# A decode step with sliding-window attention and an MLP gate: the order of the last output rows, one wide row, and 80 VectorE rows in the last key stage

## The chip, the cores and the metric

The kernel runs on one core of a Trainium2 chip. The metric is the device time of one execution in microseconds. The engines are named as the profile names them: PE is TensorE, DVE is VectorE, ACT is ScalarE, POOL is GpSimd, SP is SyncE, which issues nearly all the transfers.

## The reference, cut to what matters

One token is decoded (B = S = 1, D = 512). It is normalised, goes through attention over the last 4096 positions of 32 heads of 128, and the result is gated by a small MLP branch.

```
xn = layernorm(x)                                   # 1 x 512
q  = (xn @ wq) as 32 heads of 128
k, v = k_cache[:, :, -4096:], v_cache[:, :, -4096:]  # 32 x 4096 x 128, bf16
p  = softmax(q . k / sqrt(128))                      # per head
o  = p @ v                                           # 32 x 128
s  = o as 1 x 4096, @ wo                             # wo is 4096 x 512
h  = gelu(layernorm(xn) @ w1), its four quarters shifted along the sequence, @ w2
x1 = xn + h
g  = silu(x1 + gelu(layernorm(x1) @ w3) @ w4)        # w3 512 x 1376, w4 1376 x 512
out = x + s * g
```

With a sequence of one token the shifted quarters are all zero, so w1 is not read. Keys and values are 32 MiB each and are read once.

## The kernel before, in words

The 32 heads are worked in 8 groups of 4 (`G`). A group's keys are one tile of 128 partitions: partition b*4+a holds 128 consecutive positions of head a, 32 KB. The values lie the same way. Keys have three buffers, values two. The loop runs over stages s = 0 to 9: stage s loads and scores the keys of group s and works the values of group h = s - 2 (`LAG`). All loads go over SP's one queue in program order (`load`, line 79); a load of keys or values waits until the group that last used its buffer has been read. PE, DVE and ACT work strictly in the order in which the program lists their instructions (a manual schedule).

**Scores.** Of the 128 positions in each partition, DVE scores the first `nd(g)` and PE the rest. DVE does it in four parts (`k_vector`): a product with the broadcast query (L301) and a sum over 128 (L303). PE turns the other columns in batches of up to 8 (`k_turn`, L317), ACT copies each batch out of PSUM (L319), and PE multiplies with the query (`k_scores`, L325). `sm_own` picks each head's own score on ACT (L334); `sm_max` sums these on DVE (L339) and takes the maximum per partition (L341). `sm_turn` turns the maxima (L347 on PE; L349, L351 on DVE make `md`), and `sm_exp` broadcasts the result (L356, L359) and takes the exponentials on ACT (L363). `nd` is

```
return 64 if g < EARLY or g >= LATE else 80
```

with EARLY = 2 and LATE = 7, so group 7, whose stage is the last with keys, has 64 columns on DVE.

**Values.** `v_part` multiplies 128 columns of values with the probabilities (L423, 128 small matmuls for a group; groups 0 and 2 in another form, L415). `v_out` divides by the sum (L442 for the last two groups, L446 for others).

**Output rows.** Multiplication with wo is done in three blocks: heads 0 to 15, 16 to 23 and 24 to 31. For blocks 0 and 1 wo is loaded with eight or sixteen consecutive rows in each partition, and `ox_spread` (L453), `ox_pick` (L461, L463, L467) rearrange the attention output to match. Block 0 is a wide row (`y_wide`): 16 matmuls of 512 columns into one partition (L489), in stage 6, copied by ACT to `y_row` (L492). Block 1 is 32 narrow matmuls (`y_block` calls `rows_add`, L150), each of 128 columns[...], added up in `y_ps`. `y_row` is added to `y_ps` by `rows_add` with a one as the weight. Of the last block, 320 rows are loaded in the rearranged way into a tile of 40 used partitions (`wo_few`; `ox_few`, L473 and L476, makes its weights `of`) and the rest head by head (`wo_rows`, `y_head`).

Stage 8 closes group 7's softmax, does block 1 and `y_row`, then group 6's values, and prepares `of`. Stage 9 takes group 7's values, loaded in three pieces by `cuts = (0, 64, 112, CP)`: the first piece, then the few rows and heads 26 and 27, then the other two pieces, then heads 28 to 31. The last two DVE instructions are the gate (L602) and the residual (L604).

**MLP weights.** `w4_sb` is loaded in three transfers: 8 rows in each partition, then 2, then 96 single rows; `chunks` selects the columns of `w3_sb` to match, with steps of 8, 2 and 1.

Of the kernel before, what the change touches and what calls it, by code (L numbers as in the profile page):

```python
# [8 lines left out]
P = 128  # L9
# [3 lines left out]
ALU = mybir.AluOpType  # L13
# [8 lines left out]
NE = 5  # L22
V_BUFS = 2
EARLY = 2
LATE = 7
MOVED = (0, 2)


# [1 line left out]
def kernel(  # L30
# [14 lines left out]
    nc = tc.nc  # L45
# [9 lines left out]
    CP = G * W // P  # L55
    PB = P // G
    KC = D // P
    F = B_w3.shape[1]
    assert F == 8 * P + 2 * P + 96
    scale = float(Dh) ** -0.5  # L60


# [15 lines left out]
    def load(dst, src):  # L78
        return tc.keep_in_program_order(nc.sync.dma_start(out=dst, in_=src))
# [8 lines left out]
    w3_sb = wts.tile([P, KC, F], BF16, name="w3_sb")  # L88
    load(w3_sb[:], B_w3.rearrange("(p c) n -> p c n", p=P))
    w4_sb = wts.tile([P, 11, D], BF16, name="w4_sb")  # L90
    load(w4_sb[:, 0:8, :], B_w4[0:8 * P, :].rearrange("(p c) n -> p c n", p=P))
    load(w4_sb[:, 8:10, :], B_w4[8 * P:10 * P, :].rearrange("(p c) n -> p c n", p=P))
    load(w4_sb[0:96, 10, :], B_w4[10 * P:F, :])
    wq_sb = wts.tile([P, KC, HD], BF16, name="wq_sb")
    load(wq_sb[:], A_wq.rearrange("(p c) n -> p c n", p=P))
# [1 line left out]
    def load_kv(pool, cache, g, cuts=(0, CP)):  # L97
        t = pool.tile([P, CP, Dh], BF16, tag="kv", name="kv")
        src = cache[0, G * g:G * g + G, W0:, :].rearrange("a (b c) d -> b a (c d)", b=PB)
        dst = t[:].rearrange("p c d -> p (c d)")  # L100
        for c0, c1 in zip(cuts, cuts[1:]):
            load(dst[:, c0 * Dh:c1 * Dh], src[:, :, c0 * Dh:c1 * Dh])
        return t
# [9 lines left out]
    one_f = ones_f[0:1, 0:1]  # L113
# [33 lines left out]
    def rows_add(ps, col, w, last):  # L147
        k = col.shape[0]
        for j in range(KC):
            nc.tensor.matmul(ps[32 * j:32 * j + 1, :], lhsT=col, rhs=w[0:k, j * P:(j + 1) * P],  # L150
                             start=False, stop=last, skip_group_check=True)
# [49 lines left out]
    nc.vector.tensor_scalar(out=xn_row[:], in0=x_row[:], scalar1=negmean[:], scalar2=rstd[:],  # L201
                            op0=ALU.add, op1=ALU.mult)

    chunks = [(P, slice(r, 8 * P, 8)) for r in range(8)]
    chunks += [(P, slice(8 * P + r, 10 * P, 2)) for r in range(2)]
    chunks += [(96, slice(10 * P, F, 1))]
    a_ps = ps_misc.tile([P, 11], FP32, tag="misc", name="a_ps")
    for j, (m, cols) in enumerate(chunks):
# [50 lines left out]
    for c in range(2):  # L259
        nc.vector.tensor_copy(  # L260
            out=few[:, c, 0:4 * NE].rearrange("p (a b) -> p a b", b=4),
# [6 lines left out]
    y_ps = ps_y.tile([P, P], FP32, name="y_ps")  # L268
# [7 lines left out]
                            op=ALU.max)  # L276
    par_t = const.tile([1 + G, PB, G], FP32, name="par_t")
    nc.vector.tensor_scalar(out=par_t[:],
                            in0=ident_f[0:1 + G, 1:1 + G].unsqueeze(1).to_broadcast([1 + G, PB, G]),
# [7 lines left out]
    def nd(g):  # L287

        return 64 if g < EARLY or g >= LATE else 80

# [110 lines left out]
    def load_rows(h, n):  # L401
        if h == h_part:
            load(wo_rows[r_part:P, 0, :], A_wo[h * P + r_part:(h + 1) * P, :])
            h, n = h + 1, n - 1
        load(wo_rows[:, h - h_part:h - h_part + n, :],
             A_wo[h * P:(h + n) * P, :].rearrange("(h p) n -> p h n", p=P))
# [3 lines left out]
    def v_part(g, v, c0=0, c1=CP):  # L410
        s = st[g]
        if g in MOVED:
            s["ov"] = ps_o.tile([4 * G, 4, Dh], FP32, tag="oT", name="ov")
            for c in range(0, CP, 4):
                nc.tensor.matmul(s["ov"][:], lhsT=s["pT"][:, c:c + 4, :].rearrange("p i a -> p (i a)"),  # L415
                                 rhs=v[:, c:c + 4, :], start=(c == 0), stop=(c == CP - 4))
            s["ov_sb"] = sm_pool.tile([4 * G, 4, Dh], FP32, tag="ov_sb", bufs=1, name="ov_sb")
            nc.scalar.copy(out=s["ov_sb"][:], in_=s["ov"][:])  # L418
            return
        if c0 == 0:  # L420
            s["oT"] = ps_o.tile([P, G], FP32, tag="oT", name="oT")
        for c in range(c0, c1):
            nc.tensor.matmul(s["oT"][:], lhsT=v[:, c, :], rhs=s["pT"][:, c, :], start=(c == 0),  # L423
                             stop=(c == CP - 1))
# [46 lines left out]
    def ox_few(i):  # L471
        of_ps = ps_misc.tile([64, 8], FP32, tag="misc", name="of_ps")
        nc.tensor.matmul(of_ps[:], lhsT=few[:].rearrange("p a b -> p (a b)"), rhs=ox_blk[i][:],  # L473
                         start=True, stop=True)
        of = sm_pool.tile([64, 8], BF16, tag="of", bufs=1, name="of")
        nc.vector.tensor_copy(out=of[:], in_=of_ps[:])  # L476
        ox_blk[i] = of


    y_row = small.tile([1, D], FP32, name="y_row")  # L480

    yr = {}

    def y_wide(i, t0, t1):
        n = blocks[i][1]
        if t0 == 0:
            yr[i] = ps_tr.tile([1, D], FP32, tag="pt", name="yr_ps")
        for t in range(t0, t1):
            nc.tensor.matmul(yr[i][:], lhsT=ox_blk[i][:, t:t + 1], rhs=wo_blk[i][:, t, :], start=(t == 0),  # L489
                             stop=(t == n - 1))  # L490
        if t1 == n:
            nc.scalar.copy(out=y_row[:], in_=yr[i][:])  # L492

    def y_block(i):
        for t in range(8):
            rows_add(y_ps, ox_blk[i][:, t:t + 1], wo_blk[i][:, t, :], False)
# [2 lines left out]
        rows_add(y_ps, o_blk[few_block][:, h - few_h:h - few_h + 1], wo_row(h), h == H - 1)  # L499

    NG = H // G
    cuts = (0, 64, 112, CP)
    region = tc.manual_schedule(engines={mybir.EngineType.PE, mybir.EngineType.DVE,
                                         mybir.EngineType.Activation})
    region.__enter__()
    v_pool = None
    for s in range(NG + LAG):
        h = s - LAG
        last = h == NG - 1
        kn = load_kv(k_pool, A_k_cache, s, (0, 64, CP) if s == 0 else (0, CP)) if s < NG else None  # L510
        if s == LAG:
            wts_guard.__exit__(None, None, None)
            v_pool = ctx.enter_context(tc.tile_pool(name="v", bufs=V_BUFS))
            wo_blk[few_block] = v_pool.tile([64, 8, D], BF16, tag="wo_few", bufs=1, name="wo_few")
            nc.gpsimd.memset(wo_blk[few_block][:], 0.0)
            wo_rows = v_pool.tile([P, H - h_part, D], BF16, tag="wo_rows", bufs=1, name="wo_rows")
            nc.gpsimd.memset(wo_rows[0:r_part, 0, :], 0.0)
        if last:
            load_rows(h_part, 2)
            v = load_kv(v_pool, A_v_cache, h, cuts)  # L520
            for r, n in ((H - G, 2), (H - 2, 1), (H - 1, 1)):
                load_rows(r, n)
        elif h >= 0:
            v = load_kv(v_pool, A_v_cache, h)
        if h == 3:
            wo_24 = k_pool.tile([P, 32, D], BF16, tag="kv", name="wo_24")
            wo_blk[0], wo_blk[1] = wo_24[:, 0:16, :], wo_24[:, 16:24, :]
            load_wo(0)
        if h == 5:
            load_wo(1)  # L530
            load_few()

        if s < NG:
            nb = len(batches(s))

            def keys(b0, b1):
                for b in range(b0, b1):
                    k_turn(s, kn, b)
                    if b > 0:
                        k_scores(s, b - 1)  # L540

            k_open(s)
            k_vector(s, kn, 0)
            keys(0, 2)
            if s > 1:
                sm_den(s - 2)
                sm_rden(s - 2)
            if h - 1 in MOVED:
                v_add(h - 1)
                v_out(h - 1)  # L550
            keys(2, 4)
            k_vector(s, kn, 1)
            if s > 0:
                sm_turn(s - 1)
            if s == 6:
                ox_spread(0)
            keys(4, nb)
            k_scores(s, nb - 1)
            sm_own(s)
            if s > 0:  # L560
                sm_exp(s - 1)
            k_vector(s, kn, 2)
            if s == 6:
                ox_pick(0)
            k_vector(s, kn, 3)
            if h >= 0:
                v_part(h, v)
            sm_max(s)
            if s == 6:
                y_wide(0, 0, 16)  # L570
            if h >= 0 and h not in MOVED:
                v_out(h)
        elif s == NG:

            sm_den(NG - 2)
            sm_rden(NG - 2)
            sm_turn(NG - 1)
            ox_spread(1)
            sm_exp(NG - 1)
            ox_pick(1)  # L580
            y_block(1)
            rows_add(y_ps, one_f, y_row, False)
            v_part(h, v)
            v_out(h)
            ox_spread(few_block)
            sm_den(NG - 1)
            sm_rden(NG - 1)
            ox_pick(few_block)
            ox_few(few_block)
        else:  # L590
            v_part(h, v, 0, cuts[1])
            y_block(few_block)
            for r in range(h_part, H - G):
                y_head(r)
            for c0, c1 in zip(cuts[1:], cuts[2:]):
                v_part(h, v, c0, c1)
            v_out(h)
            for r in range(H - G, H):
                y_head(r)
# [36 lines left out]
```

## Time and profile before

| | |
|---|---|
| median of 9 runs | 194.66 us (194.46 to 195.64) |
| the profiled execution, its own time | 194.64 us |
| its span in the profile | 192.8 us |
| busy: PE, PE weight loads, DVE, ACT | 133.0, 101.6, 145.9, 85.8 us |
| read from HBM | 78.84 MB |
| mean granted PE clock | 0.685 |

The span is the time from the first to the last instruction in the profile; the 1.84 us by which the time is longer lie around it. A stage's work can be found in the timeline by the line numbers above: the last stage with keys (7) runs on DVE from 155.35 to about 170.5 us, stage 8 follows to 183.2, and stage 9 ends with L604 at 190.2 and the transfer of the output.

### The profile page before, as it was taken

Reading aid. Unit: us, or ns where it says so; the run is one execution under the profiler, and the core shown is the slowest. Engines: PE = TensorE matmul, PEld = TensorE weight load, DVE = VectorE, ACT = ScalarE, POOL = GpSimd, SP = SyncE. Lnnn points to the kernel's source line nnn. Section 1 sums busy time; section 2 is a strip of 40 time slices with the busy share of each in tenths; the row PEclk is TensorE's granted clock in tenths of the full one; section 3 lists DMA queues with packets and bytes.
Section 4 is the critical chain, followed back from the end, with each engine's and each line's share of the span. In section 5 each row is a group of like instructions: output and inputs, shape, how many; then the busy total and the mean of one; then the engine's idle time right before and its main releaser. Section 6 shows DMA issues by size and latency. Waiting matters only on the chain.

```text
span 192.8 us, 4716 instructions
## 1 busy us (share of the span) xinstructions
PE 133.0 (69%) x2098; PEld 101.6 (53%) x2098; DVE 145.9 (76%) x160; ACT 85.8 (45%) x193; POOL 6.5 (3%) x14
## 2 busy tenths in 40 slices
PE   0549763977726579778595994981788878754792
PEld 0444363866625433477584344881768257742781
DVE  1550208999999999999999999995899999950201
ACT  2003002888896360558276322771475077841000
POOL 2110008000000000000000000000000000000000
PEclk9999955589765557985558798555566696755555
DMA  5999999999999999999999999999999999999980
GB/s 187 419 476 435 398 428 432 423 428 432 435 432 435 435 430 432 435 435 435 432 432 435 428 432 404 466 435 425 421 425 437 425 435 398 449 416 396 411 336 18
DMA packets 4869, 79.13 MB, mean 410 GB/s; under 512 B 682, under 2 KB 1482, under 8 KB 1866
## 3 DMA queue, kind: packets, MB, share of 16 engines
q1 hardware_dynamic: 4698, 78.84, 96.0%
q8 instruction: 16, 0.26, 0.5%
q10 hardware_dynamic: 152, 0.00, 0.0%
q14 instruction: 3, 0.02, 0.0%
HBM read 78.84 MB, written 0.00 MB: 409 GB/s over the span
## 4 chain that ended last, share of the span: by engine, by line
DVE 42%; DMA 36%; PE 13%; ACT 5%; issue 1%; SPq 0%; ACTq 0%
DMA kv<-in_A_k_cache_dram 27%; DVE S L303 25%; DVE prod L301 14%; DMA kv<-in_A_v_cache_dram 7%; ACT kt L319 4%; PE oT L423 4%; PE pt L317 4%; PE yr_ps L489 3%; DMA x_bf<-in_A_x_dram 2%; PE sT L325 2%; PE y_ps L150 1%; DVE S L339 1%; DVE m L341 1%; DVE mx L349 1%; ACT own L334 0%
## 5 line engine op out<-in xcount | busy, mean ns | idle before, releaser
L303 DVE TENSOR_REDUCE S<-prod 128x20 f32<-128x2560 bf16 (+1 forms) x32 | 83.8, 2620 | 1.1
L319 ACT COPY kt<-pt 128x1024 bf16<-128x1024 bf16 x54 | 53.1, 1015 | 24.0 <-PE pt L317 23.4
L317 PE MATMUL pt<-ident_bf,kv 128*128 128x128 bf16 x432 | 45.8, 276 | 10.0 <-DMA kv<-in_A_k_cache_dram 7.9
L301 DVE TENSOR_TENSOR prod<-kv,q_bc 128x2560 bf16<-128x2560 bf16 (+1 forms) x32 | 44.3, 1385 | 5.5 <-DMA kv<-in_A_k_cache_dram 2.8
L317 PEld LDWEIGHTS <-kv 128*128 128x128 bf16 x432 | 36.8, 126 | 12.3 <-DMA kv<-in_A_k_cache_dram 8.8
L325 PE MATMUL sT<-qT_bf,kt 128*128 128x4 bf16 x432 | 20.1, 168 | 17.1 <-ACT kt L319 16.4
L325 PEld LDWEIGHTS <-kt 128*128 128x128 bf16 x432 | 16.8, 104 | 24.3 <-ACT kt L319 23.9
L423 PEld LDWEIGHTS <-kv 128*128 128x128 bf16 x768 | 21.0, 104 | 4.8 <-DMA kv<-in_A_v_cache_dram 4.8
L423 PE MATMUL oT<-pT,kv 128*128 128x4 bf16 x768 | 21.5, 166 | 2.9 <-DMA kv<-in_A_v_cache_dram 2.8
L415 PE MATMUL ov<-kv,pT 128*16 128x512 bf16 x64 | 18.1, 453 | 0.0
L363 ACT ACTIVATE pT<-S,mb 128x128 bf16<-128x128 f32 x32 | 13.9, 571 | 0.3
L415 PEld LDWEIGHTS <-pT 128*16 128x16 bf16 x64 | 6.4, 103 | 10.7 <-issue 5.5
L442 DVE TENSOR_TENSOR o<-oT,rden 128x4 bf16<-128x4 f32 x2 | 0.3, 162 | 13.5 <-PE oT L423 13.5
L334 ACT ACTIVATE own<-sT,par 128x48 f32<-128x48 f32 (+1 forms) x32 | 7.6, 358 | 3.6 <-PE sT L325 3.6
L446 ACT ACTIVATE o<-oT,rden 128x1 bf16<-128x1 f32 x24 | 4.3, 260 | 9.4 <-PE oT L430 5.8
L363 ACT ACTIVATION_READ_ACCUMULATOR pT<-S,mb 128x1 f32 x32 | 8.2, 257 | 0.0
L418 ACT COPY ov_sb<-ov 16x512 f32<-16x512 f32 x2 | 1.2, 576 | 14.1 <-PE ov L415 14.1
L224 DVE COPY hr<-hr_ps 1x512 f32<-1x512 f32 x1 | 0.7, 679 | 8.5 <-PE hr_ps L221 8.5
L356 PE MATMUL mb_ps<-md,par_t 5*128 5x4 f32 x16 | 3.9, 314 | 2.9 <-DVE md L351 2.2
L489 PE MATMUL yr_ps<-wo,ox 128*1 128x512 bf16 x16 | 5.0, 479 | 1.1 <-DVE ox L467 1.1
L213 ACT ACTIVATE a_bf<-a_ps 128x10 bf16<-128x10 f32 x1 | 0.2, 180 | 12.0 <-PE a_ps L210 12.0
L347 PE MATMUL mt_ps<-ident_f,m 128*1 128x128 f32 x8 | 2.8, 351 | 3.7 <-DVE rden L374 3.7
(113 smaller groups left out, 91.5 us busy)
## 6 DMA issues: line engine op xcount, KB each, us to landing
kv<-in_A_k_cache_dram SPq DMA_DIRECT2D x7, 4096.0 KB, 31.8
kv<-in_A_v_cache_dram SPq DMA_DIRECT2D x7, 4096.0 KB, 31.2
wq_sb<-in_A_wq_dram SPq DMA_DIRECT2D x1, 4096.0 KB, 18.0
kv<-in_A_k_cache_dram SPq DMA_DIRECT2D x2, 2048.0 KB, 21.5
wo<-in_A_wo_dram SPq DMA_DIRECT2D x1, 2048.0 KB, 30.7
kv<-in_A_v_cache_dram SPq DMA_DIRECT2D x1, 2048.0 KB, 13.3
kv<-in_A_v_cache_dram SPq DMA_DIRECT2D x1, 1536.0 KB, 16.4
w_sb<-in_B_w_dram SPq DMA_DIRECT2D x1, 1376.0 KB, 7.0
```

Source lines behind the costliest of these rows:

```text
L301: nc.vector.tensor_tensor(out=prod[:, 0:m, :], in0=kn[:, rows, :], in1=q_bc[:, g:g + 1, :].to_broadcast([P, m, Dh]), op=ALU.mult)
L303: nc.vector.tensor_reduce(out=st[g]["S"][:, rows], in_=prod[:, 0:m, :], axis=AX.X, op=ALU.add)
L317: nc.tensor.transpose(pt[:, c - c0, :], kn[:, c, :], ident_bf[:])
L319: nc.scalar.copy(out=kts[b][:, 0:c1 - c0, :], in_=pt[:, 0:c1 - c0, :])
L325: nc.tensor.matmul(st[g]["sT"][:, c - nd(g), :], lhsT=kt[:, c - c0, :], rhs=qT_bf[:, G * g:G * g + G], start=True, stop=True)
L334: nc.scalar.mul(s["own"][:, 0:m, a], s["sT"][:, 0:m, a], par[:, a:a + 1])
L356: nc.tensor.matmul(mb_ps[:], lhsT=par_t[:].rearrange("k b a -> k (b a)"), rhs=md[:], start=True, stop=True)
L363: nc.scalar.activation(out=s["pT"][:, :, a], in_=s["S"][:], func=ACT.Exp, scale=scale, bias=mb[:, a:a + 1], accum_out=s["sum"][:, a:a + 1])
L415: nc.tensor.matmul(s["ov"][:], lhsT=s["pT"][:, c:c + 4, :].rearrange("p i a -> p (i a)"), rhs=v[:, c:c + 4, :], start=(c == 0), stop=(c == ...
L423: nc.tensor.matmul(s["oT"][:], lhsT=v[:, c, :], rhs=s["pT"][:, c, :], start=(c == 0), stop=(c == CP - 1))
L446: nc.scalar.mul(o_blk[b][:, c + k:c + k + 1], st[g]["oT"][:, k:k + 1], st[g]["rden"][:, k:k + 1])
L489: nc.tensor.matmul(yr[i][:], lhsT=ox_blk[i][:, t:t + 1], rhs=wo_blk[i][:, t, :], start=(t == 0), stop=(t == n - 1))
```

## The change

Three things are done, beside a change of form in two places.

- LATE becomes 8: group 7 has 80 columns on DVE and 48 on PE, as groups 2 to 6 have.
- Block 1 (heads 16 to 23) is done by `y_wide` in place of `y_block`: 8 matmuls of 512 columns. DVE adds its result to `y_row`. The rows of `y_row` are added to `y_ps` after `ox_few`.
- In stage 9 the few rows and heads 26 and 27 stand ahead of all of group 7's values. `cuts` has one more entry, so that these are loaded and multiplied in four pieces (64, 32, 16, 16 columns).
- `w4` is loaded in two transfers, with 10 rows in each partition in place of 8 and 2.
- `load_kv(..., (0, CP))` spells out the default and changes nothing.

```diff
-LATE = 7
+LATE = 8
...
-    load(w4_sb[:, 0:8, :], B_w4[0:8 * P, :].rearrange("(p c) n -> p c n", p=P))
-    load(w4_sb[:, 8:10, :], B_w4[8 * P:10 * P, :].rearrange("(p c) n -> p c n", p=P))
+    load(w4_sb[:, 0:10, :], B_w4[0:10 * P, :].rearrange("(p c) n -> p c n", p=P))
...
-    chunks = [(P, slice(r, 8 * P, 8)) for r in range(8)]
-    chunks += [(P, slice(8 * P + r, 10 * P, 2)) for r in range(2)]
+    chunks = [(P, slice(r, 10 * P, 10)) for r in range(10)]
...
-        if t1 == n:
+        if i == 0:
             nc.scalar.copy(out=y_row[:], in_=yr[i][:])
+        else:
+            nc.vector.tensor_tensor(out=y_row[:], in0=yr[i][:], in1=y_row[:], op=ALU.add)
...
-    cuts = (0, 64, 112, CP)
+    cuts = (0, 64, 96, 112, CP)
...
             ox_pick(1)
-            y_block(1)
-            rows_add(y_ps, one_f, y_row, False)
+            y_wide(1, 0, 8)
             v_part(h, v)
...
             ox_few(few_block)
+            rows_add(y_ps, one_f, y_row, False)
         else:
-            v_part(h, v, 0, cuts[1])
             y_block(few_block)
             for r in range(h_part, H - G):
                 y_head(r)
-            for c0, c1 in zip(cuts[1:], cuts[2:]):
+            for c0, c1 in zip(cuts, cuts[1:]):
                 v_part(h, v, c0, c1)
```

More of the change, by code (lines that the diff above doesn't have):

```diff
@@ L58 @@
     F = B_w3.shape[1]
-    assert F == 8 * P + 2 * P + 96
+    assert F == 10 * P + 96
     scale = float(Dh) ** -0.5
@@ L523 @@
         elif h >= 0:
-            v = load_kv(v_pool, A_v_cache, h)
+            v = load_kv(v_pool, A_v_cache, h, (0, CP))
         if h == 3:
```

## Prediction

> **What bounds the kernel now.** I read the page's slices first, then the chain of waits, then the timeline from 140 us on.
>
> ```profile
> DMA  5999999999999999999999999999999999999980
> ```
>
> The 16 DMA engines are full in every slice from the second to the last but one. 78.84 MB at the 430 GB/s or so of the middle slices is about 183 us, nearly the whole span: up to its last stages the kernel is its transfers, and work that only moves inside that stretch is free. What can be lost or won lies in the last 25 us. The chain of waits says of them:
>
> ```profile
> 169.64 13.35 DMA kv<-in_A_v_cache_dram
> ```
>
> This puts the last values (group 7) down to their issue at 169.64, when PE finished group 5's values and freed the buffer. The timeline shows why that is not the release:
>
> ```profile
> 149.31 0.58 SPq L79 DMA_DIRECT2D kv<-in_A_v_cache_dram  x1
> ...
> 169.80 0.41 DVE L339 TENSOR_REDUCE S<-own 128x64 f32<-128x256 f32 x1
> ...
> 173.32 1.02 PE L150 MATMUL y_ps<-wo,ox 128*1 128x128 bf16 x32 [0.62 <-DVE ox L467]
> ...
> 177.69 3.57 PE L423 MATMUL oT<-pT,kv 128*128 128x4 bf16 x128 [2.82 <-DMA kv<-in_A_v_cache_dram]
> ...
> 183.00 0.16 DVE L476 CAST of<-of_ps 64x8 bf16<-64x8 f32 x1 [0.26 <-PE of_ps L473]
> ...
> 183.04 1.87 PE L423 MATMUL oT<-pT,kv 128*128 128x4 bf16 x64
> 184.84 1.02 PE L150 MATMUL y_ps<-wo_few,of 64*1 64x128 bf16 x32
> ...
> 186.26 0.38 PE L150 MATMUL y_ps<-wo_rows,o 128*1 128x128 bf16 x7 [0.21 <-issue]
> ...
> 186.67 1.87 PE L423 MATMUL oT<-pT,kv 128*128 128x4 bf16 x64
> ...
> 188.79 0.69 PE L150 MATMUL y_ps<-wo_rows,o 128*1 128x128 bf16 x16 [0.26 <-DVE o L442]
> ```
>
> Group 6's values were issued at 149.31 and are used at 177.69, on landing: the queue runs some 28 us behind its issues, and group 7's pieces, issued 8 us before group 6 has landed, merely stand behind it. So PE is paced by landings: 177.69 (group 6), 183.04 (first piece of group 7) and 186.67 (second). The two margins that matter: PE has issued all of row block 1 (from 173.32, then y_row until 174.88) **2.8 us** before group 6 lands, and VectorE stands idle from 173.3 to 181.3.
>
> [...]
> 1. [...] at L489, the same wide form, the weight loads at 150.78, 151.20, 151.63 and 152.06 are 0.43 us apart, and the last nine matmuls take about 2.1 us.
> 2. [...] The windows of the trace agree, and show the half clock where the change puts its wide row:
>
> ```profile
> 149.70:153.20 3.50, 2.81 (x7) 0.85 (x8) 3.43 (x4) 0.00 (x0) 0.00 (x0) 0.51 1.05 445
> 153.20:155.40 2.20, 2.18 (x11) 0.70 (x10) 1.99 (x4) 0.02 (x1) 0.00 (x0) 1.00 0.93 402
> ...
> 169.60:173.30 3.70, 1.57 (x7) 1.03 (x6) 2.03 (x9) 1.70 (x10) 0.00 (x0) 0.50 0.98 414
> 173.30:177.70 4.40, 1.56 (x41) 0.84 (x41) 0.00 (x0) 0.93 (x6) 0.00 (x0) 0.50 0.98 378
> ```
>
> Columns: stretch, its length, busy time of PE, PE weight loads, DVE, ACT and POOL, granted clock, DMA share, GB/s.
> 3. [...] The 32 narrow ones of 173.32 take 1.02 us in all, and no matmul of the trace passes another: a late wide row holds up all behind it.
> [...]
>
> **The change, part by part.**
>
> *VectorE takes 80 rows in stage 7* (LATE 8). The four parts of 16 rows become four of 20, each a product and a sum:
>
> ```profile
> L303 DVE TENSOR_REDUCE S<-prod 128x20 f32<-128x2560 bf16 x20 | 56.4, 2820 | 0.7
> L301 DVE TENSOR_TENSOR prod<-kv,q_bc 128x2560 bf16<-128x2560 bf16 x20 | 29.7, 1484 | 2.8 <-DMA kv<-in_A_k_cache_dram 2.7
> L303 DVE TENSOR_REDUCE S<-prod 128x16 f32<-128x2048 bf16 x12 | 27.4, 2286 | 0.4
> L301 DVE TENSOR_TENSOR prod<-kv,q_bc 128x2048 bf16<-128x2048 bf16 x12 | 14.6, 1220 | 2.7 <-ACT q_bc L251 2.3 <-DMA kv<-in_A_k_cache_dram 0.2
> ```
>
> 4 x (2.820 - 2.286 + 1.484 - 1.220) = 3.19 us more. VectorE runs through this stage without a gap from 155.35 to 169.80, so all of it shows. The sum of own scores shrinks to the 48-row form (0.34 for 0.41 us): -0.07. Row maximum, turn, spread, pick and ox of block 1 hang on it in one line, so **row block 1 starts at 173.32 + 3.12 = 176.44**. PE and ACT lose 16 transposes, 16 score matmuls and two of eight kt copies (2 x 1.02 us of ACT). That releases group 5's values on PE (166.09 now): they next wait for md of group 6, which VectorE gives 1.6 us later, 164.5 for 162.86. They run some 1.3 us earlier, and so does the issue of group 7's values. I cost that at nothing: the cover is group 6 in the queue until 177.69. The exponentials of group 7 end near 177.4 instead of 174.2; first use at 183 or later.
>
> *Row block 1 as a wide row.* Gone: 32 narrow matmuls (1.02 us). New: 8 of 512 columns at the half clock, 8 x 0.427 = 3.42 us[...]. They end at 176.44 + 3.42 = **179.86**. Group 6's values, queued behind on PE and landed at 177.69, start 2.17 us late. On VectorE the add into y_row (1x512; nearest rows 0.57 us of ACT at L492, 0.68 at L224) stands at about 180.2 to 180.9, ahead of the output of group 6 (181.30 + 2.17 = 183.47): hidden. The y_row copy of stage 6 stays.
>
> *y_row's rows move* from 174.28 to behind ox_few. They are 8 small f32 matmuls, 0.60 us with their drain, and fall into the wait for the of cast. That cast ends at 183.16 + 2.17 = 185.33. What is left over pushes the few rows by 0 to 0.35 us (nothing if all fits in the wait, the rest of 0.60 if not); I take 0.10, so they start at 185.45.
>
> *The few rows and two heads go ahead of group 7's values.* These matmuls are the same. Now: 184.84 to 185.79 for the few rows, to 186.67 for the heads, of which about 0.24 is the wait for the second piece. Then all 128 matmuls of the values, which have mostly landed by then: 3.57 us as at 177.69. So 185.45 + 0.95 + 0.64 + 3.57 = **190.6, where it is 188.55 now: +2.06**. The gap of about 0.4 us inside the heads has no cause in the trace; it may go or stay, 0 to -0.4. Of the last four heads the last one starts only at 189.2 now, as its rows land last; with all rows landed some 0.1 us comes back. Sum: **+1.95 us**.
>
> *Queues.* The values come in four pieces for three, not five: one issue of about 0.6 us more at 169, hidden by the 8 us of queue. SP's last wo_rows issue starts at 177.7 now, as group 6 lands, eight transfers after it: an issue seems to wait for the landing eight back. With one more piece the last two do so. They would be out by 178.6 at the latest, 10 us before use: nothing. [...] The w4 load in one issue saves SP about 0.45 us at 2 us and 128 small packets, and strides L210's weights by 10 for 8: behind it wq and the keys are queued, so 0 to -0.1. POOL's instructions don't change.
>
> The profiled execution took 194.64 us (192.8 of span and 1.84 around it), the median of the runs shown is 194.66: no correction. **194.64 + 1.95 = 196.6 us.**
>
> **Rivals.**
> - *The wide row is quick* (PE at the full clock): 8 x 0.216 = 1.73 us, over at 178.17, +0.48 at group 6. By the same sum about +0.3: 194.95, no change that can be told. Against it: clock 0.50 from 169.6 to the end, and the L489 row started at the half clock though PE had just worked. Chance 0.04.
> - *VectorE's lateness is absorbed*, or the rows don't move: the wide row starts at 173.32, ends at 176.74, before 177.69. What is left is y_row's rows in the tail, against the wait for the second piece: 194.7. The decisive point is a delay under 0.95 us. Against it: VectorE has no gap in stage 7. Chance 0.03.
> - *Faster: the chain is right*, and group 7's landing is set by its issue. That comes 1.3 us earlier: 193.3. It decides only if the queue is empty at 169.6 and the wide row is over by 177.7. For it: the chain's 13.35 us step. Against it: the DMA share of 0.98 in both windows above. Chance 0.03.
> - *The lateness as summed*, 0.90: 195.9 to 197.2, [...] the push of 0 to 0.35, and the gap of 0 to -0.4.
>
> **How the numbers follow.** A measurement of this kernel can tell about 0.3%, 0.6 us, from no change. Slower takes the last case with a little off for its low end, 0.91; same takes the first two and that end, 0.06; faster 0.03. The range 195.7 to 197.2 leaves out the three rivals and the thin ends.
>
> **What would show it.** VectorE's last L339 at about 172.9; L489's second row from 176.4 to 179.9 at clock 0.50; PE's group 6 released by PE's own row, not by the DMA; the few rows from about 185.4; no DMA wait before group 7's last pieces; L442's last at about 190.6. Group 6's values at 177.7 would prove it wrong, and a wide row under 2 us would leave the first rival.

## The result, and the profile after

The changed kernel takes 196.36 us (median of 18 runs, 195.41 to 197.77), against 194.71 us for the kernel before (median of 55). The ratio is 1.0077, 95% interval 1.0060 to 1.0094: slower by about 1.5 us. The profiled execution took 196.65 us, 0.29 us over that median, with a span of 194.9. The changed kernel's line numbers are one or two lower: it runs L421 where the kernel before ran L423, L149 for L150, L487 for L489, L301 for L303.

The lines of the timeline that answer to those of before (start, duration, engine, line, operation; in brackets the idle time ahead of it and what ended that):

```profile
172.86 0.34 DVE L337 TENSOR_REDUCE S<-own 128x48 f32<-128x192 f32 x1
...
176.32 3.57 PE L487 MATMUL yr_ps<-wo,ox 128*1 128x512 bf16 x8 [0.62 <-DVE ox L465]
...
179.83 3.40 PE L421 MATMUL oT<-pT,kv 128*128 128x4 bf16 x128
179.93 0.68 DVE L492 TENSOR_TENSOR y_row<-yr_ps,y_row 1x512 f32<-1x512 f32 x1 [3.67 <-PE yr_ps L487]
...
184.87 0.16 DVE L474 CAST of<-of_ps 64x8 bf16<-64x8 f32 x1 [0.26 <-PE of_ps L471]
...
185.29 1.42 PE L149 MATMUL y_ps<-wo_few,of 64*1 64x128 bf16 x32
...
186.64 0.38 PE L149 MATMUL y_ps<-wo_rows,o 128*1 128x128 bf16 x8
...
186.95 3.67 PE L421 MATMUL oT<-pT,kv 128*128 128x4 bf16 x128
...
190.88 0.60 PE L149 MATMUL y_ps<-wo_rows,o 128*1 128x128 bf16 x16 [0.25 <-DVE o L440]
```

VectorE closes stage 7 at 172.86 instead of 169.80. The wide row starts at 176.32 and its eight matmuls take 3.57 us; group 6's values start at 179.83 with no wait for a transfer, where they waited 2.82 us for their landing before. From there the lateness goes through to the end: the gate starts at 191.53 us, where it started at 189.53. The windows of the trace, with the clock in the third column from the end, show the wide row at half clock (0.50) and the values after it at nearly full clock (0.96):

```profile
176.30:179.80 3.50, 3.48 (x8) 0.85 (x8) 0.00 (x0) 0.91 (x6) 0.00 (x0) 0.50 1.00 368
179.80:183.30 3.50, 3.50 (x131) 3.48 (x131) 0.71 (x2) 0.00 (x0) 0.00 (x0) 0.96 0.98 365
```

So far the trace reads as the prediction does. One line doesn't fit: the 32 matmuls of the few rows (L149, `wo_few`) take 1.42 us, where they took 1.02.

### The profile page after: what moved, and what is told of

The parts are those of the page before. It is cut to its first block, busy times and chain, and to the rows that moved or that the text cites. A ratio compares the mean times of both kernels' runs of the same rounds, so it can differ in the third digit from the quotient of the medians.

```text
span 194.9 us, 4601 instructions
## 1 busy us (share of the span) xinstructions
PE 136.7 (70%) x2042; PEld 100.8 (52%) x2042; DVE 149.6 (77%) x161; ACT 83.9 (43%) x191; POOL 6.4 (3%) x14
## 4 chain that ended last, share of the span: by engine, by line
DVE 50%; DMA 29%; PE 14%; ACT 4%; issue 1%; ACTq 0%; SPq 0%
DVE S L301 29%; DMA kv<-in_A_k_cache_dram 27%; DVE prod L299 16%; PE yr_ps L487 5%; PE oT L421 4%; ACT kt L317 3%; PE pt L315 2%; DMA x_bf<-in_A_x_dram 2%; PE y_ps L149 1%; PE sT L323 1%; DVE S L337 1%; DVE mx L347 1%; DVE m L339 1%; DVE ox L465 1%; DVE md L349 1%
## 5 line engine op out<-in xcount | busy, mean ns | idle before, releaser
L301 DVE TENSOR_REDUCE S<-prod 128x20 f32<-128x2560 bf16 (+1 forms) x32 | 86.0, 2686 | 1.1
L317 ACT COPY kt<-pt 128x1024 bf16<-128x1024 bf16 x52 | 51.2, 1014 | 23.7 <-PE pt L315 23.1
L299 DVE TENSOR_TENSOR prod<-kv,q_bc 128x2560 bf16<-128x2560 bf16 (+1 forms) x32 | 45.4, 1418 | 5.5 <-DMA kv<-in_A_k_cache_dram 2.8
L323 PE MATMUL sT<-qT_bf,kt 128*128 128x4 bf16 x416 | 19.3, 168 | 14.9 <-ACT kt L317 14.1
L323 PEld LDWEIGHTS <-kt 128*128 128x128 bf16 x416 | 16.1, 105 | 22.1 <-ACT kt L317 21.8
L421 PEld LDWEIGHTS <-kv 128*128 128x128 bf16 x768 | 20.8, 102 | 1.6 <-issue 1.1
L421 PE MATMUL oT<-pT,kv 128*128 128x4 bf16 x768 | 21.2, 166 | 0.1
L413 PE MATMUL ov<-kv,pT 128*16 128x512 bf16 x64 | 19.4, 478 | 0.0
L487 PE MATMUL yr_ps<-wo,ox 128*1 128x512 bf16 x24 | 10.1, 609 | 1.8 <-DVE ox L465 1.8
L487 PEld LDWEIGHTS <-ox 128*1 128x1 bf16 x24 | 2.7, 119 | 8.3 <-issue 6.0
L440 DVE TENSOR_TENSOR o<-oT,rden 128x4 bf16<-128x4 f32 x2 | 0.3, 162 | 8.3 <-PE oT L421 8.3
```

The source lines that it names most:

```text
L299: nc.vector.tensor_tensor(out=prod[:, 0:m, :], in0=kn[:, rows, :], in1=q_bc[:, g:g + 1, :].to_broadcast([P, m, Dh]), op=ALU.mult)
L301: nc.vector.tensor_reduce(out=st[g]["S"][:, rows], in_=prod[:, 0:m, :], axis=AX.X, op=ALU.add)
L317: nc.scalar.copy(out=kts[b][:, 0:c1 - c0, :], in_=pt[:, 0:c1 - c0, :])
L323: nc.tensor.matmul(st[g]["sT"][:, c - nd(g), :], lhsT=kt[:, c - c0, :], rhs=qT_bf[:, G * g:G * g + G], start=True, stop=True)
```

## The experiments

All ratios are to the kernel before, run on the same chip at the same time. The profiled executions of e4, f2, g1 and e7 took 1.1 to 1.7 us longer than the medians of their kernels, with all of the last stages later; their lines are read for waits, not for times.

### Undoing one part, doing one part

**All but the 80 rows** (e1), the changed kernel with

```diff
-LATE = 8
+LATE = 7
```

> The changed kernel with LATE = 7, so that VectorE takes 64 rows of the last keys as before; the wide row, the late y_row rows, the order of the last rows and the four pieces stay. Theory (the two delays share one margin of 2.8 us; either alone fits into it): the wide row runs from about 173.3 to 176.7 us, group 6's values start on their landing near 177.6, and the time is back at the kernel before, ratio 0.999 to 1.002. Rival 'tail' (the late end comes from the new order and the smaller packets of the last values, whose last rows land at 190.1 in the changed kernel against 189.2 before): the time stays at 1.005 to 1.009. Rival 'additive' (each part costs its own share): about half of the 1.6 us stays, 1.003 to 1.005.

Measured: 0.9992 (0.9972 to 1.0012), 194.63 us. The wide row was over before group 6 landed, and group 6 started on its landing:

```profile
172.99 3.57 PE L487 MATMUL yr_ps<-wo,ox 128*1 128x512 bf16 x8 [0.62 <-DVE ox L465]
177.52 3.58 PE L421 MATMUL oT<-pT,kv 128*128 128x4 bf16 x128 [0.95 <-DMA kv<-in_A_v_cache_dram]
```

The wide row, the order of the last rows, the four pieces and the w4 load together cost nothing, and gain nothing, while VectorE is on time. That ends the rival 'tail', which blames the new end by itself.

**The 80 rows alone** (e2), the kernel before with

```diff
-LATE = 7
+LATE = 8
```

> The kernel before with LATE = 8 alone. Theory: VectorE is 3.1 us late, block 1 as narrow rows starts at 176.4 and with y_row is issued by 178.0, so group 6's values start about 0.3 us late; ratio 1.000 to 1.003. Rival 'additive': VectorE's 3.1 us cost about half of the loss, 1.004 or more. Rival 'tail': 1.000, VectorE does not matter.

Measured: 1.0053 (1.0033 to 1.0074), 196.01 us. That is more than my theory allowed, and within the range of the rival 'additive'; but e1, where that rival expected 1.003 to 1.005, speaks against it.

**The change with narrow rows** (e3), the changed kernel with

```diff
-            y_wide(1, 0, 8)
+            y_block(1)
```

> The changed kernel with block 1 as 32 narrow matmuls again in place of the wide row (y_row then holds block 0 alone, its rows are still added after ox_few); 80 rows on VectorE and the new tail stay. Theory: block 1 starts at 176.3 and is issued by 177.4, before group 6 lands near 177.6; ratio 0.999 to 1.002. Rival 'additive': 1.003 to 1.005. Rival 'tail': 1.005 to 1.009.

Measured: 1.0078 (1.0055 to 1.0101), 196.51 us: no better for taking away the very thing that the prediction blames.

**The wide row alone** (e4), the kernel before with `y_wide(1, 0, 8)` in place of `y_block(1)`, VectorE's add, and y_row's rows after `ox_few`.

> The kernel before with the wide row alone (added to y_row by VectorE; y_row's rows moved behind ox_few, as in the change), 64 rows on VectorE, the tail as before. Theory: the wide row ends at 176.7, before group 6 lands; y_row's rows fall into the wait for the of cast; ratio 0.999 to 1.002. Rival 'additive': 1.003 to 1.005. Rival 'tail': 1.000.

Measured: 1.000 (0.9982 to 1.0018), 194.70 us, as expected.

So the loss hangs on the 80 rows, and with them it is there with the wide row or without. What takes its place is in e3's timeline. Group 6 starts on its landing at 177.60, and then:

```profile
183.33 0.26 PE L149 MATMUL y_ps<-wo_few,of 64*1 64x128 bf16 x1
183.85 1.02 PE L149 MATMUL y_ps<-wo_few,of 64*1 64x128 bf16 x31 [0.26 <-issue]
184.80 0.38 PE L149 MATMUL y_ps<-wo_rows,o 128*1 128x128 bf16 x8
185.11 2.53 PE L421 MATMUL oT<-pT,kv 128*128 128x4 bf16 x89
189.23 1.20 PE L421 MATMUL oT<-pT,kv 128*128 128x4 bf16 x39 [1.58 <-issue]
```

PE stands still for 1.58 us in the middle of 128 equal matmuls, within the second of the four pieces, whose values had landed at 185.77. "issue" means that it waited for nothing that the profile shows. A shorter gap of 0.26 us lies exactly 31 + 8 + 89 = 128 matmuls earlier. The chain of waits of e2 has the same gap, again with 39 matmuls of group 7 to go:

```profile
186.51 0.83 PE oT L423 x25
187.34 1.02 issue
188.35 1.22 PE oT L423 x39
```

A matmul goes with a weight load (the page of the kernel before counts 2098 of each); I call the two a pair. The same page lists a queue by the name of instruction, 0.26 MB in 16 packets, 16 KB each:

```profile
q8 instruction: 16, 0.26, 0.5%
```

PE's 2098 pairs go with 16 packets, one for 131 pairs; 2042 pairs (the changed kernel) go with 16, one for 128, and 2194 (f6, below) with 17, one for 129. That is close to the 128 matmuls between the two gaps. That PE waits in the gap of 1.58 us for such a packet was my estimate from these counts and from the times below; it was not shown. Nor is it shown whether busy DMA engines are the reason: in e3's trace their share is 0.95 from 183.0 to 186.7 us, but 0.56 from 186.7 to 189.2, where the packet ends (187.74) and the gap after it.

Counted from the start of PE's program, all of PE's gaps of 0.2 us or more that are put down to "issue", in the traces of all fourteen kernels, stand at five places: pairs 223, 862, 1245, 1883 (or 1884) and 2011. Within 4 pairs these are whole multiples of 128 apart. All 45 of these gaps end 1.2 to 1.6 us after a packet of that queue, be they 0.2 or 2.8 us long. Which of them show differs from kernel to kernel. The kernel before has three gaps: 0.87 us ending at 28.52, 2.09 us ending at 95.73, both far ahead of the last stages, and 0.21 us (0.40 between two weight loads) ending at 186.26, inside the heads 26 and 27.

### Moving the place

First I took the place of the gap in PE's program for the cause. Idle pairs of a weight load and a matmul of 4 columns move it. They were put at the end of stage 5, where PE waits for keys at 131 us:

```diff
+            if s == 5:
+                idle(32)      # 96 in the third run
             sm_max(s)
```

**The 80 rows alone, with 32 idle pairs** (f1).

> The kernel before with LATE = 8 alone (the run that took 1.0053), and 32 pairs of a weight load and a small matmul of 4 columns put where PE idles at 131 us, so that PE's program is as long as before again (the rows that left PE are 32 pairs). Theory 'fetch' (VectorE's lateness is still inside the margin; what costs 1 us is a gap in group 7's values at a fixed place of PE's program, pair 2011 of 2066, 55 pairs from the end[...]; 32 more pairs move that place to 87 pairs from the end): no such gap in group 7's values, ratio 0.999 to 1.002. Rival 'rows' (80 rows on VectorE cost it by themselves): 1.004 to 1.007, gap or not.

Measured: 1.0094 (1.0058 to 1.0131), 196.83 us. Not cured. (That it is worse than e2 is not shown; the intervals overlap.)

**The narrow-row kernel with 32 idle pairs** (f2).

> The changed kernel with the narrow rows for block 1 (the run that took 1.0078) and the same 32 idle pairs. Theory 'fetch': the gap of 1.7 us in group 7's values goes, ratio 0.999 to 1.002. Rival 'rows' or 'tail' (80 rows, or the new order and packets of the tail): stays at 1.006 to 1.009.

Measured: 1.0099 (1.0061 to 1.0137). Not cured either.

**The kernel before with 96 idle pairs** (f6). From the distances of 128 I estimated that 96 pairs more move the gaps in PE's program to where 32 fewer do.

> The kernel before, nothing of the change, with 96 idle pairs of a weight load and a small matmul at 131 us. [...] Theory 'fetch': a gap of about 1 us or more in group 7's values, ratio 1.003 to 1.008, with no VectorE lateness at all. Rival 'rows': 0.999 to 1.001, since 2.6 us of PE in an idle place are free.

Measured: 0.9994 (0.9976 to 1.0011). Free: no gap in the last stages, though the places moved.

All three expectations of 'fetch' as a matter of place failed. The gaps did move, as seen from the work that they interrupt. In f1, whose program is as long as that of the kernel before, the gap of group 7 is gone and a longer one stands in group 6, in the chain of waits:

```profile
180.76 2.76 issue
183.52 0.88 PE oT L423 x27
```

The place alone doesn't decide, then. The next theory was that it takes both the place and **the time at which PE passes the matmul 128 pairs before it**. In the expectations it goes by the name 'late PE, late instructions'; that PE waits for instructions is a guess in this name, and was not shown. In f1 the gap stands 128 pairs after a matmul in the middle of row block 1, and that row block is late with VectorE, at 176.42 for 173.32.

**Half the wide row** (e8), the changed kernel with

```diff
-            y_wide(1, 0, 8)
+            y_wide(1, 0, 4)      # and stop at t == t1 - 1
```

> The changed kernel with 4 of the 8 matmuls of the wide row of block 1 left out (half of that block's part of the output is missing). My prediction's theory 'late wide row alone': PE is 1.7 us earlier at group 6's values (about 178.1) and the end follows, ratio 1.000 to 1.003. Theory 'wide row, and the fetch behind it': group 6 starts at 178.1, but group 7's values then meet the gap that the narrow-row run showed, at pair 2011 of 2038, and the end comes back to within 0.5 us of the changed kernel's: 1.004 to 1.008.

Measured: 1.0034 (1.0014 to 1.0053), a little under the range of the second theory and just above that of the first. Group 6 started at 178.90 in its trace and group 7's values had a gap of 0.76 us. A shorter wide row does help, but it gives back only about half of the loss.

### VectorE alone

**The 80 rows with VectorE on time** (g1): e2's program on PE, instruction by instruction, with a fifth of VectorE's scores of group 7 set to zero.

```diff
+        if g == 7:
+            nc.vector.memset(st[g]["S"][:, m * part + 16:m * part + m], 0.0)
+            m = 16
+            rows = slice(20 * part, 20 * part + m)
```

> The kernel before with LATE = 8 (the run that took 1.0053), with the last 4 of the 20 rows of each of VectorE's four parts in stage 7 left out and set to zero, so that PE's program is the same instruction by instruction and only VectorE is on time again. Theory 'late PE, late instructions' [...]: 0.999 to 1.001. Rival 'program' (PE's program with 64 instructions fewer meets the gap wherever VectorE is): 1.004 to 1.007.

Measured: 1.0001 (0.9982 to 1.0021), and no gap:

```profile
174.45 1.02 PE L150 MATMUL y_ps<-wo,ox 128*1 128x128 bf16 x32 [0.62 <-DVE ox L471]
175.41 0.60 PE L150 MATMUL y_ps<-y_row,ones_f 1*1 1x128 f32 x8
179.00 3.57 PE L427 MATMUL oT<-pT,kv 128*128 128x4 bf16 x128 [3.00 <-DMA kv<-in_A_v_cache_dram]
```

PE's program is acquitted: with VectorE on time the same instructions cost nothing. Then the reverse: **the kernel before, PE's program unchanged, with VectorE late** by one (g2) or two (g3) unused products of 1.22 us after its last part in stage 7.

```diff
             k_vector(s, kn, 3)
+            if s == 7:      # g3: the product twice
+                late = prod_pool.tile([P, 20, Dh], BF16, tag="prod", name="late")
+                nc.vector.tensor_tensor(out=late[:, 0:16, :], in0=kn[:, 0:16, :],
+                                        in1=q_bc[:, s:s + 1, :].to_broadcast([P, 16, Dh]), op=ALU.mult)
```

> The kernel before with one more product of 16 rows (1.22 us) on VectorE after the last part of stage 7, its result unused; PE's program is unchanged. Theory 'late PE, late instructions': [...] 1.2 us later PE waits some 0.8 us there; ratio 1.002 to 1.005. My prediction's margin of 2.8 us: free, 0.999 to 1.001.

> As the run with one more product, with two (2.44 us). Theory 'late PE, late instructions': a gap of about 2 us in group 6's values, ratio 1.006 to 1.010. My prediction's margin of 2.8 us: row block 1 and y_row are issued by 177.4, before group 6 lands, and the time is that of before, 0.999 to 1.001.

Measured: g2 1.0023 (0.9994 to 1.0053), which can't be told from no change; g3 1.0083 (1.0054 to 1.0112), which can. g3 shows it best. It has nothing of the change, and by the prediction's margin it would be free. In its timeline

```profile
175.65 1.02 PE L150 MATMUL y_ps<-wo,ox 128*1 128x128 bf16 x32 [0.62 <-DVE ox L467]
176.60 0.60 PE L150 MATMUL y_ps<-y_row,ones_f 1*1 1x128 f32 x8
177.69 2.88 PE L423 MATMUL oT<-pT,kv 128*128 128x4 bf16 x102 [0.48 <-DMA kv<-in_A_v_cache_dram]
182.41 0.85 PE L423 MATMUL oT<-pT,kv 128*128 128x4 bf16 x26 [1.84 <-issue]
```

group 6 starts at 177.69, to the hundredth where it started before: the margin was there. But after 102 of its 128 matmuls PE stops for 1.84 us. In g2 it stops at the same place for 0.41 us. In the kernel before it passes there without a stop.

The DMA records of the traces put a packet of the instruction queue ahead of each of these gaps:

| kernel | packet ends | gap ends | between |
|---|---|---|---|
| g2 | 179.59 | 181.12 | 1.5 |
| g3 | 180.95 | 182.41 | 1.5 |
| f1 | 182.04 | 183.52 | 1.5 |
| f2 | 183.01 | 184.62 | 1.6 |
| e2 | 187.06 | 188.35 | 1.3 |
| e3 | 187.74 | 189.23 | 1.5 |

The packet follows VectorE: for the place inside group 6 it ends at 178.70 in the kernel before, 179.59 in g2 and 180.95 in g3, while group 6 starts at 177.69, 177.83 and 177.69. With 1.5 us added, an estimate from the table, a gap at this place would end at about 180.2 in the kernel before; PE gets there at 177.69 + 102 x 0.0275 = 180.5 us (3.52 us for 128, as at 145.76). By this sum the margin was about 0.3 us, not 2.8. It gives gaps of 0.9 and 2.1 us for 1.22 and 2.44 us of lateness; measured are 0.41 and 1.84, which put the margin at 0.8 and 0.6.

**The wide row at full clock** (e7), the changed kernel with unused wide matmuls where PE waits for VectorE.

```diff
+            warm(16, 0)
             sm_den(NG - 2)
...
             ox_pick(1)
+            warm(2, 0)
```

> The changed kernel with 18 unused wide matmuls on PE where it waits for VectorE in stage 8 (16 ahead of the turn, 2 ahead of the wide row), to have the clock released before the wide row. If it is, the wide row takes 1.7 us for 3.4 and group 6's values start near 178.1. The rival of my prediction, 'quick wide row': ratio 1.000 to 1.003. Theory 'late PE, late instructions': [...] 1.003 to 1.008.

Measured: 1.0087 (1.0061 to 1.0114), just above the range of the second theory. The eight matmuls of the wide row took 1.89 us for 3.57, and the kernel is no better for it. In e7's trace seven weight loads of the unused matmuls in a row, from 170.65 to 173.21, stand 0.43 us apart, and the next seven take 1.38 us in all. That is the pace of clock 1.00 in the kernel before: the last eight weight loads of L489 there, from 153.24, take 1.59 us in all, 0.216 us apart, and the clock is 1.00 from 153.20 to 155.40. With the 18 added pairs PE has 2060 for 2042, and it stops at pair 2011, in group 7 after 95 of its matmuls:

```profile
178.40 1.89 PE L487 MATMUL yr_ps<-wo,ox 128*1 128x512 bf16 x8
...
186.92 2.69 PE L421 MATMUL oT<-pT,kv 128*128 128x4 bf16 x95
191.05 1.04 PE L421 MATMUL oT<-pT,kv 128*128 128x4 bf16 x33 [1.44 <-issue]
```

With a quick wide row 1.7 us of the row are gone and the gap of 1.44 us stands in their place, as with the narrow rows of e3. No version tried beats the kernel before; e1 and e4 equal it.

## Why the prediction was right, and where it was not

**VectorE's 3.12 us**: right. The sum of the own scores (L339, now L337) came 3.06 us later (172.86 for 169.80) and the wide row started at 176.32, 0.12 us before the forecast.

**The wide row's 3.42 us at the half clock**: right (3.57 us with the end of the last matmul, at clock 0.50). Group 6 started at 179.83, forecast 179.86.

**From there to the end**: right in sum, by terms that cancel, which is luck. Forecast was that group 7's values end at 190.6, and L440 followed them at 190.66. But PE ran group 6 at nearly full clock (0.96; 3.40 us for 3.57), and `of` ended at 185.03, 0.30 us before the forecast of 185.33. The gap of 0.4 us inside the heads, for which I found no cause and which I let go or stay, went, and one like it (0.43 us between two weight loads) came up inside the few rows. Both fit the gaps shown above: the first ends 1.5 us after a packet of the instruction queue, at pair 2011, the second 1.5 us after another, at pair 1883; the changed program has 56 pairs fewer (2042 for 2098), so that other work stands at these places. y_row's rows cost about 0.2 us for the 0.10 taken: the few rows start 0.26 us after `of`, where PE elsewhere follows VectorE within about 0.06 (190.66 + 0.16 to 190.88). Of the last four heads, 0.1 us was to come back; the gate's L601 starts 2.00 us later, forecast 1.95. The medians, 196.36 and 194.71, lie 1.65 us apart: the traced execution, which the forecast met, is slower than the median.

**The rival 'VectorE's lateness is absorbed'**: its arithmetic for a wide row on time was right (e1: 194.63 us, forecast 194.7). **'The wide row is quick'**: its sum gave 194.95, but with a row of 1.89 us (e7) the kernel took 196.94, so this sum lacks the same term as the margin below. **Queues**: nothing that can be told was paid for the fourth piece, the later issues (in the changed kernel the last two of `wo_rows` started at 177.57 and 177.95 us) or the w4 load (e1). **"Full" engines**: the page's DMA row has an 8, not a 9, in the last slice but one; nothing in the forecast hangs on it.

**The step that failed is the margin.** "PE has issued all of row block 1 ... 2.8 us before group 6 lands" treats those 2.8 us as free, and with it 'a delay under 0.95 us' as the point for the wide row. For data they are free, as g3's start at 177.69 shows; all in all only 0.3 to 0.8 us were, by the packet and by the gaps of g2 and g3. Two consequences that I drew in the expectations were therefore wrong. The narrow rows were to bring the time back (e3: they did not), and the 80 rows alone were to cost next to nothing (e2: 1.0053). And "idle" was taken for "not needed": where the wait before group 6's landing shrank from 2.82 us to 0.48 (g3), the gap of 1.84 us came up. That such a wait gives instructions time to arrive is a guess; it was not shown. The number was right because in the changed kernel the wide row's lateness is the delay that shows in the trace, as forecast. That a second delay of about the same size stands behind it, ready to take its place, I did not see.

**Shown**: VectorE's lateness alone, with PE's program unchanged, costs the time (g3); the program alone does not (g1, f6); gaps lie multiples of 128 pairs apart, but for up to 4, and end 1.2 to 1.6 us after a packet of the instruction queue, and the packet moves with VectorE (g2, g3). **Argued, not shown**: that PE waits for that packet. No run was without these packets, and the profile doesn't show when one is asked for, or by which engine. From PE's matmul 128 pairs before a gap to the end of the gap 4.6 us (e8) to 6.8 us (f1) go by; what sets that is open. It is not simply that this matmul sets off the packet for the place 128 pairs on: in e1 the packet starts at 177.22 and that matmul, the sixth of group 6, at 177.68. So it is in e4, f6 and g1 too, where PE stood waiting for a landing just ahead of that place. In e2, where PE came to the same matmul without a wait, the packet started 2.2 us after it (179.93 for 177.69).

## What to carry to other kernels

A wait ahead of a landing is not spare until a run has used it up: here 0.3 to 0.8 us were free of 2.82, by the estimates from the packet and from g2 and g3. Look for gaps put down to "issue", count the pairs of weight load and matmul between two of them, and compare with the packets of the instruction queue. No run here tried to leave PE a pause in the last stages for every 128 pairs, or to use fewer and larger matmuls there; that either would help is a guess from the distances of the gaps. When a sum comes out right, take its main term away on the chip before you believe it; here the time stayed.

## What the runs showed of the hardware that I had not expected

- The traces list packets of a queue named instruction, 16 KB each: 16 for PE's 2098 pairs in the kernel before, 16 for 2042 in the changed one, 17 for 2194 in f6. PE's gaps ended 4.6 (e8) to 6.8 us (f1) after the matmul 128 pairs before them, while PE ran 128 small pairs in 3.52 to 3.57 us in the kernel before (145.76 and 177.69).
- After the wide matmuls PE's clock was higher for the 128 small ones (0.96 from 179.80 to 183.30), and these took 3.40 us, for 3.57 at clock 0.50 in the kernel before (from 177.69): small matmuls hardly gained from the clock here.
- 96 pairs of weight load and small matmul in an idle place of PE cost nothing (0.9994), and with VectorE late 32 such pairs at the same place moved the gap from group 7 to group 6 (f1); they did not bring back the time.
